# lam spread over partitions by a product with ones, and another order of the first weight chunks

## The chip, the cores and the metric

The kernel runs on one core of a Trainium2 chip. The metric is the device time of one execution, in microseconds (us), as the median of several runs. One further execution is recorded by the hardware profiler; all rows below are from that one.

## The reference, cut to what matters

The program is a linear attention with decay followed by two feed-forward layers, all in 32-bit floats. Inputs are q, k and v of 2 batches, 8 heads, 768 positions and 64 dimensions, one decay lam per head, and two pairs of weights.

```python
# per head, blocks of positions with a running state kv:
intra = (q_b @ k_b.T) * Dmask            # Dmask[i, j] = lam ** (i - j) for i >= j, else 0
out_b = intra @ v_b + (q_b * lam ** (pos + 1)) @ kv
kv    = lam ** block * kv + (k_b * lam ** (block - 1 - pos)).T @ v_b
x = out reshaped to 1536 tokens x 512
# layer 1 (w_in 512 x 2048, w_out 2048 x 512), ELU:
h = x @ w_in;  g = where(h > 0, h, exp(min(h, 0)) - 1);  x = g @ w_out
# layer 2, leaky with one slope alpha per hidden unit:
h = x @ w_in;  g = max(h, 0) + alpha * min(h, 0);         x = g @ w_out
```

## The kernel before, in words

The attention works on 12 blocks of 128 positions (6 per batch), all 8 heads of a block together. For block n, `scores(n)` (L201) multiplies keys and queries into two PSUM banks, `mask(n)` (L208, VectorE) multiplies them with the decay matrix `dm` into SBUF, `state(n)` (L223) multiplies the decayed keys `kd` (L182, GpSimd) with the values, `new_state(n)` (L235 ScalarE, L239 and L241 VectorE) updates the running state, and `outputs(n)` (L256 and, except in the first block of a batch, L262) adds what the block gives and what the state gives. `keep(n)` splits the output into a high part (L274, ScalarE) and a remainder (L275, VectorE), because the feed-forward products are made of three products of such parts in a reduced format.

The feed-forward part is a list of 96 items: layer, quarter of the hidden units, tile of 512 tokens, 128 hidden units. `up(i)` (L359) is 12 matmuls, then ScalarE's relu and exp (L370, L373), VectorE's `g` (L374), ScalarE's high part `gh` (L380) and GpSimd's remainder `gl` (L381). `down(i)` (L397) is 12 matmuls into four banks and runs two items later (`LAG`). PSUM has 8 banks in a ring, so a bank is reused once the tile eight allocations earlier is read.

Weights arrive in chunks of 1 MB. Chunk c = 2n is up weights (`wih`, `wil`) and c = 2n + 1 down weights (`woh`, `wol`) of the n-th pair of hidden units' groups: items 0 and 1 use chunk 0 in `up` and chunk 1 in `down`; items 2 and 3 use chunks 2 and 3. Three raw buffers hold them as they come. `split_w` converts one in six steps: a scaling on ScalarE (L125), a shift and two combining steps on VectorE (L126, L128, L131), the high part on ScalarE (L134) and the remainder on GpSimd (L135).

The order of each engine's instructions is the order in which they are written (`manual_schedule`); each engine works its own list in that order and waits where an operand isn't ready. A counter sets where a step of `split_w` stands: `tick()` advances it and issues what is due, `later(n, step)` makes a step due n ticks on. A block of the first four has three ticks between `block_a` and `block_b` and three behind; `up` has four, and an item four more in its `down`. So `split_w(c, gaps, first)` gives the ticks of the six steps, counted from where it is called:

```python
later(first, ...)     # ScalarE: scaling
later(gaps[0], ...)   # VectorE: shift
later(gaps[1], ...)   # VectorE: combining 1
later(gaps[2], ...)   # VectorE: combining 2
later(gaps[3], ...)   # ScalarE: high part
later(gaps[4], ...)   # GpSimd: remainder
```

`begin()` holds the start: lam is read three times in copies over partitions (L301, L304), blocks 0 to 3 and chunk 0 are loaded on SP's queue, PE runs up with 8 products of zeros (L281), and `dm` and `qp` (powers of lam) are built with scans on VectorE (L325, L330). The first four blocks (`AHEAD`) run by themselves; the other eight are laced into items 0 to 7, one each. `load(n + 4)` is issued behind block n, which frees its buffer, and `load_w` at places of its own, all on SP's queue.

Of the kernel before, what the change touches and what calls it, by code (L numbers as in the profile page):

```python
# [7 lines left out]
F32 = mybir.dt.float32  # L8
# [3 lines left out]
ALU = mybir.AluOpType  # L12

B, H, S, D = 2, 8, 768, 64
# [3 lines left out]
NP = H // 2  # L18
# [8 lines left out]
NG = 4  # L27
GF = NF // NG
LAG = 2
WARM = 8  # L30
AHEAD = 4


# [1 line left out]
def attention_two_layers(  # L35
# [13 lines left out]
    nc = tc.nc  # L49
# [3 lines left out]
    tiny = ctx.enter_context(tc.tile_pool(name="tiny", bufs=1))  # L53
# [12 lines left out]
    def bank(name):  # L66
        return ps.tile([128, 512], F32, tag="ps", name=name)

    alpha_sb = tiny.tile([128, NF], F32, name="alpha_sb")
    beta = tiny.tile([128, NF], F32, name="beta")  # L70
    warm = tiny.tile([128, C], F32, name="warm")
    anti = tiny.tile([128, C], F32, name="anti")
    lam_sb = tiny.tile([128, H], F32, name="lam_sb")
    lamp = tiny.tile([128, H], F32, name="lamp")
    fill = tiny.tile([128, 176], F32, name="fill")


    clock = [0]
# [2 lines left out]
    def later(n, step):  # L81
        if n:
            due.setdefault(clock[0] + n, []).append(step)
        else:
            step()
# [11 lines left out]
    def load_w(c):  # L97
        n, part = divmod(c, 2)
        l, k = divmod(n, NPAIR)
        wi, wo = wts[l]  # L100
        r = wraw.tile([128, 2048], U32, tag="raw", name="raw")
        if part == 0:
            nc.sync.dma_start(
                out=r.rearrange("p (c f) -> p c f", c=NCC),
                in_=wi[:, k * 512:(k + 1) * 512].rearrange("(c p) f -> p c f", p=128))
        else:
            nc.sync.dma_start(
                out=r.rearrange("p (f e) -> p f e", f=2),
                in_=wo[k * 256:(k + 1) * 256, :].rearrange("(f p) e -> p f e", p=128))
        raw[c] = r  # L110

    def split_w(c, gaps=(5, 6, 8, 11, 13), first=3):
        n, part = divmod(c, 2)
        r = raw.pop(c).rearrange("p (f w) -> p f w", w=2)


        upper, lower = r[:, :, 1], r[:, :, 0]
        t = wt.tile([128, 1024], F32, tag="wt", name="wt")
        tu = t.bitcast(U32)
        tag = "wi" if part == 0 else "wo"  # L120
        h = wsp.tile([128, 1024], F32R, tag=tag + "h", name=tag + "h")
        lo = wsp.tile([128, 1024], F32R, tag=tag + "l", name=tag + "l")
        shape = dict(c=NCC) if part == 0 else dict(c=2)
        split[c] = [x.rearrange("p (c f) -> p c f", **shape) for x in (h, lo)]
        later(first, lambda: nc.scalar.mul(t, upper.bitcast(F32), 2.0 ** -112))  # L125
        later(gaps[0], lambda: nc.vector.tensor_scalar(  # L126
            out=tu, in0=tu, scalar1=3, scalar2=None, op0=ALU.logical_shift_left))
        later(gaps[1], lambda: nc.vector.scalar_tensor_tensor(  # L128
            out=tu, in0=lower, scalar=29, in1=tu,
            op0=ALU.logical_shift_right, op1=ALU.bitwise_or))  # L130
        later(gaps[2], lambda: nc.vector.scalar_tensor_tensor(  # L131
            out=tu, in0=upper, scalar=0x80000000, in1=tu,
            op0=ALU.bitwise_and, op1=ALU.bitwise_or))
        later(gaps[3], lambda: nc.scalar.copy(h, t))  # L134
        later(gaps[4], lambda: nc.gpsimd.tensor_tensor(  # L135
            out=lo, in0=t, in1=h.bitcast(F32), op=ALU.subtract))
# [24 lines left out]
    def load(n):  # L161


        t = accp.tile([128, 4, 512], F32, tag="acc", name="blk")
        z = t[:, 0:2].rearrange("p s (a i) -> p s a i", a=NP)
        nc.sync.dma_start(out=z, in_=kqT[n])
        m = 2 if n % PB != PB - 1 else 1
        u = t[:, 2:4].rearrange("p s (h d) -> p s h d", h=H)
        nc.sync.dma_start(
            out=u[:, 0:m], in_=vk[n, :, 0:m, :].rearrange("j a (h d) -> j a h d", h=H))  # L170
        ld[n] = z
        vs[n] = (u[:, 0], u[:, 1] if m > 1 else None)
# [21 lines left out]
    def scores(n):  # L194
        z = ld[n]

        ps_ = [bank("sc"), bank("sc")]
        for pr in range(NP):
            for hs in range(2):
                a, b = hs * 64, (hs + 1) * 64  # L200
                nc.tensor.matmul(  # L201
                    out=ps_[hs][:, pr * C:(pr + 1) * C], lhsT=z[a:b, 0, pr, :],
                    rhs=z[a:b, 1, pr, :], start=True, stop=True)
        sc[n] = ps_

    def mask(n):
        for hs, p_ in enumerate(sc.pop(n)):
            nc.vector.tensor_tensor(  # L208
                out=sms[n % 2][:, hs], in0=p_.rearrange("p (a i) -> p a i", a=NP),
                in1=dm[:, hs], op=ALU.mult)  # L210
# [64 lines left out]
        nc.vector.tensor_tensor(  # L275
            out=xl[t][:, :, o:o + C], in0=pv, in1=xh_.bitcast(F32), op=ALU.subtract)

    def run_up():
        pw = bank("warm")
        for _ in range(WARM):  # L280
            nc.tensor.matmul(out=pw[:, 0:C], lhsT=warm, rhs=warm, start=True, stop=True)  # L281

    def block_a(n):
        p_ = state(n)
        if n + 1 < NBLK:
            scores(n + 1)
            mask(n + 1)
        return p_
# [8 lines left out]
            scale(n + 2)  # L297

    def begin():

        nc.sync.dma_start(out=lam_sb, in_=bass.AP(  # L301
            tensor=lam.tensor, offset=lam.offset, ap=[[0, 128], [1, H]]))
        for hs in range(2):
            nc.scalar.dma_start(out=lamp[hs * 64:(hs + 1) * 64, 0:NP], in_=bass.AP(  # L304
                tensor=lam.tensor, offset=lam.offset + hs, ap=[[0, 64], [2, NP]]))
        load(0)
        nc.scalar.dma_start(out=alpha_sb, in_=alpha)
        load(1)
        load_w(0)
        load(2)  # L310
        load(3)
        nc.vector.memset(warm, 0.0)
        run_up()

        nc.gpsimd.memset(anti, 0.0)
        nc.gpsimd.affine_select(
            out=anti, in_=anti, pattern=[[1, C]], base=1 - C, channel_multiplier=1,
            compare_op=ALU.not_equal, fill=1.0)
        nc.scalar.activation(fill[:, 0:1], warm[:, 0:1], AF.Exp)


        for hs in range(2):
            for pr in range(NP):
                h = 2 * pr + hs
                nc.vector.tensor_tensor_scan(  # L325
                    out=dm[:, hs, pr, :], data0=lam_sb[:, h:h + 1].to_broadcast([128, C]),
                    data1=anti, initial=0.0, op0=ALU.mult, op1=ALU.add)

        for pr in range(NP):
            nc.vector.tensor_tensor_scan(  # L330
                out=qp[:, pr, :], data0=lamp[:, pr:pr + 1].to_broadcast([128, C]),
                data1=warm, initial=1.0, op0=ALU.mult, op1=ALU.add)
        for s_ in st:
            nc.gpsimd.memset(s_, 0.0)
        scores(0)
        nc.vector.tensor_scalar(
            out=beta, in0=alpha_sb, scalar1=-1.0, scalar2=1.0, op0=ALU.mult, op1=ALU.add)
        scale(0)
        mask(0)
        scale(1)  # L340
        split_w(0, (3, 4, 5, 8, 9), 2)


    gh = {}
# [83 lines left out]
             for l in range(2) for q in range(NG) for t in range(NCH) for j in range(GF)]  # L428
    PER = NCH * GF

    when = {-1: [1], 0: [2], 2: [3]}
    early = {1: ((8, 9, 10, 12, 14), 7), 2: ((5, 6, 8, 9, 11), 2)}
    for g in range(1, 2 * NG):
        o = (g - 1) * PER

        a, b = (7, 8) if g == 1 else (2, 5)
# [3 lines left out]
    def weights(i):  # L440
        for c in when.get(i, []):
            split_w(c, *early.get(c, ()))
            if c + 3 < 4 * NPAIR:
                later(12 if c == 1 else 9, lambda c=c: load_w(c + 3))

    def parts(i, e):

# [3 lines left out]

    with tc.manual_schedule():
        begin()
        for n in range(AHEAD):
            weights(n - AHEAD)
            p_ = block_a(n)
            for _ in range(3):
                tick()
            block_b(n, p_)
            if n < 2:  # L460
                load_w(1 + n)
            if n == 3:
                load_w(3)
            for _ in range(3):
                tick()
        for i, _ in enumerate(items):
            n = AHEAD + i
            p_ = block_a(n) if n < NBLK else None
            up(i)
            weights(i)  # L470
            if n < NBLK:
                block_b(n, p_)
            for e in range(4):
                if i < LAG:
                    tick()
                else:
                    for c0, c1 in parts(i - LAG, e):
                        down(i - LAG, e, c0, c1)
        for i in range(len(items) - LAG, len(items)):
            for e in range(4):  # L480
                for c0, c1 in parts(i, e):
                    down(i, e, c0, c1)
# [50 lines left out]
```

## Time and profile before

| | us |
|---|---|
| median of 3 runs | 595.18 (594.75 to 597.2) |
| the profiled execution | 595.87 |
| its span, first to last instruction | 594.1 |
| PE (matmul) busy | 577.2, 97% of the span |
| VectorE (DVE) busy | 273.5, 46% |
| ScalarE (ACT) busy | 241.1, 41% |
| GpSimd (POOL) busy | 228.4, 38% |

Shares of busy time are averages over the whole span. The granted clock is TensorE's as a share of 2.4 GHz; its mean over the span is 0.986. A row of the chain of waits says what the work that ended last was waiting for or doing at that time. L12 is line 12 of the kernel before.

### The profile page before, as it was taken

How to read it: one execution, taken by the hardware profiler on the slowest of the kernel's cores; microseconds unless marked ns; L12 is line 12 of the kernel's file. 1: busy time of each engine (PE TensorE's matmuls, PEld its weight loads, DVE VectorE, ACT ScalarE, POOL GpSimd, SP SyncE). 2: the span in 40 equal slices, each digit the busy share in tenths (PEclk: the TensorE clock that was granted, in tenths of full speed). 3: DMA queues.
4: the chain of work that ended last, by engine and by line, in shares of the span. 5: the costliest groups of instructions: out<-in, count | busy, mean ns of one | idle time of the engine just before them, and what ended most of it. 6: DMA issues, size and time to landing. Idle time of an engine off the chain costs nothing.

```text
span 594.1 us, 7308 instructions
## 1 busy us (share of the span) xinstructions
PE 577.2 (97%) x2956; PEld 477.3 (80%) x2956; DVE 273.5 (46%) x359; ACT 241.1 (41%) x374; POOL 228.4 (38%) x156
## 2 busy tenths in 40 slices
PE   4897999999999999999999999999999999999997
PEld 4785778888888888888888888888888888888886
DVE  3786532656425435535526643443435532551332
ACT  1462444465445445454546533443324232422220
POOL 2648431354443443253344434353323344332211
PEclk7897999999999999999999999999999999999999
DMA  5995500242122222041022222122202110000111
GB/s 195 406 352 180 180 1 1 72 141 72 71 72 71 72 71 72 0 135 40 38 71 72 71 72 71 54 91 71 68 3 84 59 72 0 2 0 1 71 72 71
DMA packets 18993, 49.24 MB, mean 83 GB/s; under 512 B 1936, under 2 KB 2192, under 8 KB 18960
## 3 DMA queue, kind: packets, MB, share of 16 engines
q1 hardware_dynamic: 18272, 48.77, 23.6%
q8 instruction: 23, 0.38, 0.2%
q10 hardware_dynamic: 688, 0.01, 0.1%
q14 instruction: 10, 0.08, 0.0%
HBM read 45.63 MB, written 3.15 MB: 82 GB/s over the span
## 4 chain that ended last, share of the span: by engine, by line
PE 92%; DVE 3%; DMA 3%; ACT 1%; issue 0%; DVEq 0%; POOL 0%; POOLq 0%
PE up L359 44%; PE dn L397 44%; DMA raw<-in_w1i 2%; PE po L262 1%; PE po L256 1%; PE sc L201 1%; DMA lamp<-in_lam 1%; DVE wt L128 1%; DVE wt L131 1%; PE stp L223 1%; DVE acc L413 0%; ACT st L235 0%; ACT wt L125 0%; ACT wih L134 0%; DVE st L241 0%; DVE wt L126 0%
## 5 line engine op out<-in xcount | busy, mean ns | idle before, releaser
L381 POOL TENSOR_TENSOR gl_t<-g_t,gh_t 128x512 fp32r<-128x512 f32 x96 | 125.2, 1304 | 327.1 <-ACT gh_t L380 274.5
L370 ACT ACTIVATE r_t<-up 128x512 f32<-128x512 f32 x96 | 57.3, 597 | 197.0 <-PE up L359 197.0
L380 ACT CAST gh_t<-g_t 128x512 fp32r<-128x512 f32 x96 | 59.6, 621 | 108.8 <-DVE g_t L374 55.7
L413 DVE TENSOR_TENSOR acc<-dn,acc 128x512 f32<-128x512 f32 (+1 forms) x73 | 46.9, 676 | 75.7 <-PE dn L397 75.7
L397 PE MATMUL dn<-woh,gl_t 128*128 128x512 f32 (+1 forms) x196 | 75.4, 385 | 0.0
L397 PE MATMUL dn<-woh,gh_t 128*128 128x512 f32 (+1 forms) x196 | 75.4, 385 | 0.0
L397 PE MATMUL dn<-wol,gh_t 128*128 128x512 f32 (+1 forms) x196 | 75.4, 385 | 0.0
L378 DVE SCALAR_TENSOR_TENSOR g_t<-r_t,beta,up 128x512 f32<-128x512 f32 x48 | 35.7, 743 | 86.2 <-ACT r_t L370 77.5
L397 PE MATMUL dn<-gh_t,woh 128*128 128x512 f32 x192 | 75.3, 392 | 0.0
L397 PE MATMUL dn<-gl_t,woh 128*128 128x512 f32 x192 | 74.8, 389 | 0.0
L397 PE MATMUL dn<-gh_t,wol 128*128 128x512 f32 x192 | 74.7, 389 | 0.0
L374 DVE SCALAR_TENSOR_TENSOR g_t<-r_t,up 128x512 f32<-128x512 f32 x48 | 32.8, 683 | 63.1 <-ACT r_t L373 63.1
L359 PE MATMUL up<-xh,wih 128*128 128x512 f32 x192 | 53.1, 399 | 3.7 <-ACT wih L134 3.7
L359 PE MATMUL up<-xh,wil 128*128 128x512 f32 x192 | 52.2, 394 | 0.0
L359 PE MATMUL up<-xl,wih 128*128 128x512 f32 x192 | 52.2, 394 | 0.0
L359 PE MATMUL up<-yh,wih 128*128 128x512 f32 x192 | 51.3, 389 | 0.0
L359 PE MATMUL up<-yl,wih 128*128 128x512 f32 x192 | 51.3, 389 | 0.0
L359 PE MATMUL up<-yh,wil 128*128 128x512 f32 x192 | 51.3, 389 | 0.0
L359 PEld LDWEIGHTS up<-xh,wih 128*128 128x128 f32 x192 | 36.0, 190 | 11.8 <-ACT wih L134 3.9
L126 DVE TENSOR_SCALAR wt<-wt 128x1024 uint32<-128x1024 uint32 x32 | 30.0, 938 | 31.9 <-ACT wt L125 31.9
L359 PEld LDWEIGHTS up<-xh,wil 128*128 128x128 f32 x192 | 36.6, 191 | 7.8
L359 PEld LDWEIGHTS up<-xl,wih 128*128 128x128 f32 x192 | 36.6, 191 | 7.8
(52 smaller groups left out, 800.0 us busy)
## 6 DMA issues: line engine op xcount, KB each, us to landing
raw<-in_w1i SPq DMA_DIRECT2D x8, 1024.0 KB, 5.9
raw<-in_w1o SPq DMA_DIRECT2D x8, 1024.0 KB, 5.0
raw<-in_w2i SPq DMA_DIRECT2D x8, 1024.0 KB, 5.4
raw<-in_w2o SPq DMA_DIRECT2D x8, 1024.0 KB, 4.8
blk<-in_kqT SPq DMA_DIRECT2D x12, 512.0 KB, 6.1
blk<-in_vk SPq DMA_DIRECT2D x10, 512.0 KB, 7.0
out<-acc SPq DMA_DIRECT2D x11, 256.0 KB, 2.0
blk<-in_vk SPq DMA_DIRECT2D x2, 256.0 KB, 5.9
```

The lines of the kernel that those rows point to most:

```text
L126: later(gaps[0], lambda: nc.vector.tensor_scalar(out=tu, in0=tu, scalar1=3, scalar2=None, op0=ALU.logical_shift_left))
L128: later(gaps[1], lambda: nc.vector.scalar_tensor_tensor(out=tu, in0=lower, scalar=29, in1=tu, op0=ALU.logical_shift_right, op1=ALU.bitwise ...
L131: later(gaps[2], lambda: nc.vector.scalar_tensor_tensor(out=tu, in0=upper, scalar=0x80000000, in1=tu, op0=ALU.bitwise_and, op1=ALU.bitwise ...
L201: nc.tensor.matmul(out=ps_[hs][:, pr * C:(pr + 1) * C], lhsT=z[a:b, 0, pr, :], rhs=z[a:b, 1, pr, :], start=True, stop=True)
L359: nc.tensor.matmul(out=p_, lhsT=w[:, cc, fo:fo + 128], rhs=x[t][:, cc, :], start=n == 0, stop=n == 3 * NCC - 1)
L370: nc.scalar.activation(r, p_, AF.Relu, scale=-1.0)
L374: later(1, lambda: nc.vector.scalar_tensor_tensor(out=g, in0=r, scalar=-1.0, in1=p_, op0=ALU.add, op1=ALU.max))
L378: later(1, lambda: nc.vector.scalar_tensor_tensor(out=g, in0=r, scalar=beta[:, f:f + 1], in1=p_, op0=ALU.mult, op1=ALU.add))
L380: later(2, lambda: nc.scalar.copy(gh_, g))
L381: later(3, lambda: nc.gpsimd.tensor_tensor(out=gl_, in0=g, in1=gh_.bitcast(F32), op=ALU.subtract))
L397: nc.tensor.matmul(out=p_, lhsT=a, rhs=b, start=first and n == 0, stop=last and n == 2)
L413: nc.vector.tensor_tensor(out=a, in0=p_, in1=a, op=ALU.add)
```

## The change

lam is read once, as one row of 8 numbers on one partition. A matmul of a row of ones with it puts it on all 128 partitions; three copies on VectorE bring it into `lam_sb` and, for each half of the partitions, its even or odd heads into `lamp`. The run-up is three products ahead of that matmul and six behind it. alpha is loaded on SP's queue at item 2, and beta is made from it at item 20; both were in `begin()`. The conversion of chunk 0 has its first step one block later. Chunk 2 is loaded and converted ahead of chunk 1: its load comes behind block 0 and its conversion is called ahead of block 3; chunk 1's load comes behind block 1 and its conversion is called in item 0. `fill` is made smaller, so that the new row finds room.

```diff
-WARM = 8
...
+    row = tiny.tile([1, 128 + H], F32, name="row")
-    fill = tiny.tile([128, 176], F32, name="fill")
+    fill = tiny.tile([128, 40], F32, name="fill")
...
-    def run_up():
+    def run_up(n):
         pw = bank("warm")
-        for _ in range(WARM):
+        for _ in range(n):
             nc.tensor.matmul(out=pw[:, 0:C], lhsT=warm, rhs=warm, start=True, stop=True)
...
     def begin():
-        nc.sync.dma_start(out=lam_sb, in_=bass.AP(
-            tensor=lam.tensor, offset=lam.offset, ap=[[0, 128], [1, H]]))
-        for hs in range(2):
-            nc.scalar.dma_start(out=lamp[hs * 64:(hs + 1) * 64, 0:NP], in_=bass.AP(
-                tensor=lam.tensor, offset=lam.offset + hs, ap=[[0, 64], [2, NP]]))
+        nc.sync.dma_start(out=row[:, 128:128 + H], in_=lam.rearrange("h a -> a h"))
         load(0)
-        nc.scalar.dma_start(out=alpha_sb, in_=alpha)
         load(1)
         load_w(0)
         load(2)
         load(3)
         nc.vector.memset(warm, 0.0)
-        run_up()
+        nc.vector.memset(row[:, 0:128], 1.0)
...
+        run_up(3)
+
+        p_ = bank("lamp")
+        nc.tensor.matmul(
+            out=p_[:, 0:H], lhsT=row[:, 0:128], rhs=row[:, 128:128 + H], start=True, stop=True)
+        run_up(6)
+        nc.vector.tensor_copy(lam_sb, p_[:, 0:H])
+        for hs in range(2):
+            a, b = hs * 64, (hs + 1) * 64
+            nc.vector.tensor_copy(
+                lamp[a:b, 0:NP], lam_sb.rearrange("p (a s) -> p s a", s=2)[a:b, hs])
...
         scores(0)
-        nc.vector.tensor_scalar(
-            out=beta, in0=alpha_sb, scalar1=-1.0, scalar2=1.0, op0=ALU.mult, op1=ALU.add)
         scale(0)
         mask(0)
         scale(1)
-        split_w(0, (3, 4, 5, 8, 9), 2)
+        split_w(0, (5, 6, 7, 9, 11), 4)
...
-    when = {-1: [1], 0: [2], 2: [3]}
-    early = {1: ((8, 9, 10, 12, 14), 7), 2: ((5, 6, 8, 9, 11), 2)}
+    when = {-1: [2], 0: [1], 2: [3]}
+    early = {2: ((4, 5, 6, 8, 10), 3), 1: ((3, 4, 5, 7, 9), 2)}
...
-                later(12 if c == 1 else 9, lambda c=c: load_w(c + 3))
+                later(9, lambda c=c: load_w(c + 3))
...
             if n < 2:
-                load_w(1 + n)
+                load_w(2 - n)
...
         for i, _ in enumerate(items):
+            if i == 2:
+                nc.sync.dma_start(out=alpha_sb, in_=alpha)
+            if i == 20:
+                nc.vector.tensor_scalar(
+                    out=beta, in0=alpha_sb, scalar1=-1.0, scalar2=1.0, op0=ALU.mult,
+                    op1=ALU.add)
             n = AHEAD + i
```

## Rows read from the trace of the kernel before

**Rows 1.** The page's chain that ended last: shares of the span by engine.
```profile
PE 92%; DVE 3%; DMA 3%; ACT 1%; issue 0%; DVEq 0%; POOL 0%; POOLq 0%
```
**Rows 2.** Busy us of each engine in stretches, then granted clock, DMA share, GB/s.
```profile
5.00:10.00 5.00, 1.49 (x14) 1.50 (x16) 1.04 (x4) 0.83 (x2) 0.00 (x0) 0.86 0.50 183
10.00:15.00 5.00, 2.17 (x26) 1.76 (x26) 3.28 (x7) 0.00 (x0) 1.57 (x2) 0.50 1.03 405
15.00:20.00 5.00, 5.00 (x63) 4.71 (x60) 3.11 (x7) 1.74 (x2) 2.18 (x3) 0.62 1.03 420
...
100.00:580.00 480.00, 480.00 (x2137) 397.48 (x2136) 212.21 (x263) 201.06 (x296) 180.88 (x117) 1.00 0.18 60
```
**Rows 3.** The same view in stretches of 1 us, at 49 us.
```profile
49.00:50.00 1.00, 0.00 (x0) 0.00 (x0) 1.00 (x2) 0.23 (x1) 1.00 (x1) 0.78 0.08 33
```
**Rows 4.** Chain of waits in order of time, 0 to 60 us: start, us, what.
```profile
7.15 9.95 DMA raw<-in_w1i
...
17.12 1.15 ACT wt L125
...
24.09 1.04 ACT wih L134
...
27.38 1.14 PE po L262 x8
...
34.24 2.96 PE up L359 x12
...
42.42 1.16 ACT wt L125
...
44.47 3.28 DVE wt L128
...
49.77 1.05 ACT wih L134
...
50.87 5.49 PE up L359 x12
```
**Rows 5.** Timeline of PE: start, us, instructions, count [idle before, releaser].
```profile
8.51 2.03 PE L201 MATMUL sc<-blk 64*128 64x128 f32 x16 [3.67 <-DMA blk<-in_kqT]
...
16.43 1.97 PE L256 MATMUL po<-sm,blk 128*64 128x128 f32 x16
...
45.99 1.16 PE L201 MATMUL sc<-blk 64*128 64x128 f32 x16
```
**Rows 6.** Timeline of SP's queue: the issue of block 0's first half.
```profile
1.18 0.42 SPq L166 DMA_DIRECT2D blk<-in_kqT  x1
```
**Rows 7.** Transfers of tile blk issued in 56 to 60 us: issue to landing.
```profile
DMA to landing us min/median/max: 3.3/3.7/4.2
```
**Rows 8.** The page's DMA queues: packets, MB, share; this is ACT's queue.
```profile
q10 hardware_dynamic: 688, 0.01, 0.1%
```
**Rows 9.** Timeline of DVE: start, us, instructions, count [idle before, releaser].
```profile
3.41 2.63 DVE L325 TENSOR_TENSOR_SCAN dm<-lam_sb,anti 128x128 f32<-128x128 f32 x8 [2.41 <-DMA lam_sb<-in_lam]
11.72 2.19 DVE L330 TENSOR_TENSOR_SCAN qp<-lamp,warm 128x128 f32<-128x128 f32 x4 [5.67 <-DMA lamp<-in_lam]
...
13.88 1.28 DVE L208 TENSOR_TENSOR sm<-sc,dm 128x512 f32<-128x512 f32 x2
...
18.90 0.85 DVE L239 COPY st<-stp 64x256 f32<-64x256 f32 x2
19.79 0.69 DVE L275 TENSOR_TENSOR xl<-po,xh 128x512 fp32r<-128x512 f32 x1
...
36.69 1.22 DVE L128 SCALAR_TENSOR_TENSOR wt<-raw,wt 128x1024 uint32<-128x1024 uint32 x1
```
**Rows 10.** Timeline of POOL: start, us, instructions, count.
```profile
46.61 2.04 POOL L182 TENSOR_TENSOR kd_t<-blk,dm 128x512 f32<-128x512 f32 x1
...
71.68 2.41 POOL L135 TENSOR_TENSOR wol<-wt,woh 128x1024 fp32r<-128x1024 f32 x1
74.03 1.07 POOL L182 TENSOR_TENSOR kd_t<-blk,dm 128x512 f32<-128x512 f32 x1
```

## The prediction

> **What bounds the kernel now.** I read the chain of waits by engine and the busy times per stretch first. The chain lies on TensorE (PE) for 92% of the span [rows 1], and PE is busy for the whole of 100 to 580 us [rows 2]. Nothing in the change touches that part: the same matmuls run there behind the same conversions. So a gain or a loss must come from the first 60 us, and I read those in the chain of waits in order of time and then engine by engine.
>
> The chain there has three links to see [rows 4]. First, the first weight chunk (c = 0) is issued at 7.15 and lands 9.95 us later, at 17.1. Second, its conversion runs from 17.12 over ScalarE (ACT) and VectorE (DVE) to the copy at 24.09; the state update of block 1 is queued behind that copy, and PE's matmuls with this state start only at 27.38. From there PE runs with hardly a wait through up(0), 34.24 to 37.20. I call the end of up(0) U; it is 37.2. Third, chunk 2 (the second chunk of up weights): its conversion starts at 42.42 and ends with the copy at 49.77; PE has been idle since 47.15 [rows 5] and starts up(2) at 50.87. In that idle time the granted clock began to fall to its lower level, 1.2 of 2.4 GHz (0.78 on average in 49 to 50) [rows 3], and up(2) takes 5.49 us where up(0) took 2.96 [rows 4].
>
> Ahead of all this lies the transfer stream. It moves 183 GB/s between 5 and 10 us and 405 GB/s from 10 on [rows 2], and the first block, issued at 1.18 [rows 6], lets PE start at 8.51 only [rows 5].
>
> **The change part by part.** Times are of the profiled execution, 595.87 us.
>
> *lam as one row.* Three small transfers go (one of lam on SP, two on ACT), and alpha's leaves ACT's queue. Added are one row of 8 numbers, a memset of one row, a product with ones on PE, and three small DVE copies. The row stands first on SP, as lam does today, which has landed when the scans start at 3.41 [rows 9]; the trace doesn't show the row's own landing, and I take 3.4. For the product I take 0.4: a pair of f32 matmul records is 0.15 (16 in 1.16) at the full clock and 0.25 at the low one [rows 5], plus a hand-over. Each copy is at most one scan of 128 columns, 2.63/8 = 0.33 [rows 9], so 0 to 1.0 together, I take 0.6; the memset runs while DVE waits for the row. The eight scans then run from 4.4 to 7.0, and the four of qp follow at once to 9.2 with their 2.19, where today they wait for the transfer until 11.72. mask(0) ends at 10.5 with 1.28 [rows 9]. Of the run-up three products stand ahead of the lam product and six behind; these end at about 6.5 and delay only scores(0), which mask(0) doesn't need before 9.2.
>
> *The stream.* What I expect from this part is an earlier stream. The only sign in the trace is time: with the second queue's 688 small packets [rows 8] in flight the stream ran at less than half of its later rate [rows 2]. With an empty queue a block half lands 3.3 us after its issue [rows 7]; 0.52 MB at 405 GB/s are 1.3 of these. Block 0's first half, issued at 1.18, would then land at 4.5. Chunk 0 is the fifth load on SP, 3.15 MB with those ahead of it, 7.8 us of stream: it lands at 1.2 + 2.0 + 7.8 = 11.0. I allow 0.8 for a slow start and take 11.8 instead of 17.1. The bounds are 11.0 and the 17.1 of today.
>
> *Conversion of chunk 0 behind the first block.* Its first step (ACT) now stands behind ACT's copy of block 0's output, and its shift (DVE) behind mask(1), the state copies and the subtraction of block 0. So it can't start before that output: mask(0) at 10.5, the output matmuls (1.97 at the low clock [rows 5], half of it at the full one), one ACT copy (0.6, as half of the 1.04 for twice the columns [rows 4]): 12.1 to 13.1. From the start of the first step to the copy takes 6.97 today (17.12 to 24.09) [rows 4]; two state copies and a subtraction, 0.85 + 0.69, leave this stretch and mask(2), 1.28, comes in [rows 9]: 6.7. From the copy's start to the state matmuls of block 2 is 3.29 (24.09 to 27.38). So these start at 22.1 to 23.1 instead of 27.38. I take 23.1, since PE starts at the low clock: **4.2 us earlier**. The upper bound is 5.2. The lower is a stream as late as today: block 0's output at 18.4 (16.43 + 1.97) then holds the first step until 19.0, so the state matmuls come at 19.0 + 6.7 + 3.3 = 29.0, 1.6 later than today. Behind the shift that waits for chunk 0 DVE has mask(2), state(1) and mask(3) queued, so PE waits there in any case; at the full clock it would idle from 19 to 22.
>
> From there to U PE has its 9.8 us as today (27.38 to 37.20); the conversion of chunk 2, begun in block 3, lies beside it on ACT and DVE, and its last DVE step comes about when up(0) ends.
>
> *Up weights ahead of down weights.* Chunk 2 is loaded and converted before chunk 1. up(2) would start 9.9 behind U (47.15 − 37.20), and chunk 2 is done 1 to 4 us behind U, so the wait of 50.87 − 47.15 = 3.7 goes, and with it the low clock's 5.49 − 2.96 = 2.5: **6.2 us**. What is late next is chunk 1, the first down weights. Its conversion takes the very place that chunk 2's has today, behind item 0's g on ACT, 5.2 behind U (42.42 − 37.20). There chunk 2 was done with the copy 13.6 behind U (49.77 + 1.05). Its last two DVE steps took 5.3 (44.47 to 49.77) instead of 2 x 1.22 [rows 4, 9], while GpSimd (POOL) ran a subtraction, a kd and a qs product beside them (kd 2.04 instead of 1.07) [rows 10]. With only kd and qs beside them they take some 1.4 less (estimate); mask(6) now stands between them and costs some 0.7 net. So woh is ready 12.9 to 14.1 behind U (the later where the copy of chunk 2 holds up item 0's relu by up to 1.2), and wol 2.41 later [rows 10], at 15.3 to 16.5. down(0) comes at 9.9 + 2.96 + 1.0 = 13.9 and wants wol 0.45 later; its second bank waits for item 1's g, whose ACT steps queue behind woh, some 3 us after it (estimate: item 0's set with a state update took the 5.2 above). **New wait: 2.4 us**, bounds 0.5 (DVE undisturbed) and 6.3 (3.8, and the clock falling as at 49 to 50 for another 2.5). Chunks 3 and on keep their places.
>
> The trace shows a DVE step of two SBUF inputs stretched from 1.22 to 3.28 beside POOL [rows 4, 9]. The Trainium skill (SBUF — State Buffer, "Who interferes with whom") says that such an instruction shares a read interface with a GpSimd one that reads SBUF, and that one of them then blocks for the other's whole instruction. By that rule each step could wait out kd or qs in full and the new wait would be some 3.5; with the undisturbed 1.22 it would be 0.5. The rows lean to the rule.
>
> *alpha and beta.* alpha's issue moves to SP at item 2, behind a weight load that waits for chunk 1's buffer, and ahead of block 10's loads, needed three items later; beta (16 columns on DVE) to item 20. beta is used from item 48 on. PE's chain passes neither: 0; without that cover it would be one issue, 0.4 us [rows 6].
>
> **Sum.** 4.2 + 6.2 − 2.4 = 8.0 us: 595.87 − 8.0 = 587.9. The profiled execution is 0.7 above the median of the runs, 595.18, so I predict 587.2.
>
> **Rivals.**
> *The stream stays late* (it is slow at first by itself). For it: the second queue carried few bytes while the stream moved 183 GB/s [rows 2, 8]. Against it: an idle queue lands a block half in 3.3 us [rows 7]. Then −1.6 + 6.2 − 2.4 = 2.2: 593.0. The Trainium skill (DMA: Bandwidth & Descriptors, "Issuing engines are not separate DMA queues") says that all DMAs run on the same 16 engines and that issuing from several engines saves only issue time; by that rule leaving ACT's queue empty would give this rival's time, and the trace of before doesn't decide it.
> *The new wait is long*: woh late, PE idle long enough that the clock falls. 4.2 + 6.2 − 6.3 = 4.1: 591.1. For it: the clock fell 2.4 us into the idle time that begins at 47.15 [rows 3, 5]. Against it: the wait is cut in pieces by the matmuls with woh.
> *All fits*: 5.2 + 6.2 − 0.5 = 10.9: 584.3.
> *Slower, by the clock*: PE idles at the state matmuls of block 2, the clock falls there, and the gaps up to down(0) keep it low. Every us at the low level costs 0.43 to 0.5 (1.16 against 2.03 for scores) [rows 5]. It decides from 16 us of low clock on; 20 us give 595.2 − 8.0 + 10 = 597.2. For it: one spell, about 8.6 to 18.8, lasted 10 us (0.86, 0.50 and 0.62 in three stretches) [rows 2]. Against it: it ended once PE had work without gaps.
>
> **How the numbers follow.** Forecast 0.52, stream late 0.13, long wait 0.16, all fits 0.14, slower 0.05. The range goes from 582.5 (all fits, and 1.8 more for what the low clock cost before up(0)) to 593.5 (stream late, and 0.5 more wait). Half a per cent, what a measurement of this kernel tells from no change, is 3 us: faster (below 592.2) is the forecast, all fits, most of the long wait and a third of the late stream, 0.85; the same 0.11; slower 0.04.
>
> **What would show it.** Right: scores(0) start before 7 us, chunk 0's first step at 12 to 14, up(0) ends near 33, no wait of up(2), and waits of 1 to 4 us at down(0), first on wol or woh. Wrong: the stream's rate in 5 to 10 still near 183 GB/s; a granted clock below 1 behind 20 us; a wait of up(2); any new PE wait behind 70 us.

## The result, and the profile after

The changed kernel takes 587.08 us (median of 4 runs, 586.05 to 587.99) beside 596.19 us for the kernel before on the same chip (4 runs): a ratio of 0.9848, 95% interval 0.9815 to 0.9880. The profiled execution took 586.05 us with a span of 584.1; that of before took 595.87 with 594.1.

The stream of large loads starts at once. The stretches of the kernel after, with busy us of PE, PE's weight loads, DVE, ACT and POOL, then the granted clock, DMA share and GB/s, as in [rows 2]:

```profile
5.00:10.00 5.00, 4.97 (x60) 4.17 (x60) 5.00 (x12) 0.00 (x0) 1.47 (x2) 1.00 0.96 358
10.00:15.00 5.00, 2.73 (x44) 2.52 (x42) 4.01 (x7) 1.71 (x2) 1.95 (x3) 0.89 1.04 416
15.00:20.00 5.00, 5.00 (x62) 4.30 (x60) 3.20 (x4) 1.47 (x3) 4.95 (x4) 0.77 1.03 409
```

358 GB/s in 5 to 10 us stand against 183. Chunk 0 is also issued earlier, at 2.96 instead of 7.15. In the kernel before, the chain of waits begins with one of lamp's two transfers, and chunk 0's issue comes behind its landing (start, us, what):

```profile
0.74 6.39 DMA lamp<-in_lam
7.13 0.02 issue
7.15 9.95 DMA raw<-in_w1i
```

SP's queue waited twice for lamp to land, once with a half of block 2 (L169) and once with chunk 0 (L103); the kernel after has no such wait (us in total, times, longest):

```profile
SPq L169 <- DMA lamp<-in_lam: 2.6, 1, 2.6
...
SPq L103 <- DMA lamp<-in_lam: 1.1, 1, 1.1
```

The clock, recorded as low from 8.6 to 18.8 before, is recorded as low only from about 14 to 17 (0.89 and 0.77 in two stretches). PE's timeline (start, us, instructions, idle time before and what ended it) answers to [rows 5]; I add the steps at which the chain of the first 50 us can be read:

```profile
2.63 0.59 PE L317 MATMUL lamp<-row 1*128 1x8 f32 x2
...
6.01 1.65 PE L201 MATMUL sc<-blk 64*128 64x128 f32 x16
...
13.68 1.93 PE L201 MATMUL sc<-blk 64*128 64x128 f32 x16 [2.27 <-DMA blk<-in_kqT]
...
20.19 1.09 PE L256 MATMUL po<-sm,blk 128*64 128x128 f32 x16
21.82 1.13 PE L262 MATMUL po<-qs_t,st 128*128 128x128 f32 x8 [0.53 <-DVE st L241]
...
28.40 1.20 PE L362 MATMUL up<-xh,wih 128*128 128x512 f32 x4
...
41.33 1.19 PE L362 MATMUL up<-xh,wih 128*128 128x512 f32 x4
...
45.66 0.40 PE L400 MATMUL dn<-gl_t,woh 128*128 128x512 f32 x1
47.33 0.50 PE L400 MATMUL dn<-gh_t,wol 128*128 128x512 f32 x1 [1.28 <-POOL wol L135]
```

scores(0) start at 6.01 instead of 8.51, the state matmuls of block 2 at 21.82 instead of 27.38 [rows 4], up(0) at 28.40 instead of 34.24. up(2), at 41.33, has no wait. The 12 matmuls of the first down(0) begin at 45.3 and stop after two of them: the third wants `wol` and waits 1.28 us. All waits of PE, longest first (us in total, times, longest):

```profile
PE sc L201 <- DMA blk<-in_kqT: 2.3, 1, 2.3
PE dn L400 <- POOL wol L135: 1.3, 1, 1.3
PE warm L281 <- DVE warm L306: 1.1, 1, 1.1
PE po L262 <- DVE st L241: 0.5, 1, 0.5
```

VectorE's side of the start, and of chunk 1's conversion (answers to [rows 9]):

```profile
3.26 0.17 DVE L320 COPY lam_sb<-lamp 128x8 f32<-128x8 f32 x1 [2.13 <-PE lamp L317]
...
3.83 2.63 DVE L330 TENSOR_TENSOR_SCAN dm<-lam_sb,anti 128x128 f32<-128x128 f32 x8
6.38 2.16 DVE L335 TENSOR_TENSOR_SCAN qp<-lamp,warm 128x128 f32<-128x128 f32 x4
8.47 2.45 DVE L208 TENSOR_TENSOR sm<-sc,dm 128x512 f32<-128x512 f32 x4
...
20.79 0.88 DVE L241 TENSOR_TENSOR st<-stp,st 64x256 f32<-64x256 f32 x2 [2.29 <-ACT st L235]
...
39.47 1.96 DVE L128 SCALAR_TENSOR_TENSOR wt<-raw,wt 128x1024 uint32<-128x1024 uint32 x1
41.35 1.27 DVE L208 TENSOR_TENSOR sm<-sc,dm 128x512 f32<-128x512 f32 x2
42.55 1.21 DVE L131 SCALAR_TENSOR_TENSOR wt<-raw,wt 128x1024 uint32<-128x1024 uint32 x1
```

The copy of the lam product starts at 3.26, the scans follow without a wait, and the masks of blocks 0 and 1 begin at 8.47 instead of 13.88. ScalarE, where the first conversion begins behind the copy of block 0's output, and ends ahead of the state update:

```profile
10.90 0.58 ACT L274 CAST xh<-po 128x512 fp32r<-128x512 f32 x1 [8.67 <-PE po L256]
12.16 1.12 ACT L125 ACTIVATE wt<-raw 128x1024 f32<-128x1024 f32 x1 [0.68 <-DMA raw<-in_w1i]
18.53 1.05 ACT L134 CAST wih<-wt 128x1024 fp32r<-128x1024 f32 x1 [5.25 <-DVE wt L131]
...
43.80 1.05 ACT L134 CAST woh<-wt 128x1024 fp32r<-128x1024 f32 x1 [5.19 <-DVE wt L131]
```

and GpSimd beside chunk 1's conversion (answers to [rows 10]):

```profile
38.84 1.50 POOL L182 TENSOR_TENSOR kd_t<-blk,dm 128x512 f32<-128x512 f32 x1
40.31 2.27 POOL L189 TENSOR_TENSOR qs_t<-blk,qp 128x512 f32<-128x512 f32 x1
44.92 2.36 POOL L135 TENSOR_TENSOR wol<-wt,woh 128x1024 fp32r<-128x1024 f32 x1 [2.34 <-ACT woh L134]
```

### The profile page after: what moved, and what is told of

It reads as the page before. It is cut to its first block, busy times and chain, and to the rows that moved or that the text cites. A ratio compares the mean times of both kernels' runs of the same rounds, so it can differ in the third digit from the quotient of the medians.

```text
span 584.1 us, 7319 instructions
## 1 busy us (share of the span) xinstructions
PE 575.3 (98%) x2960; PEld 475.6 (81%) x2960; DVE 271.8 (47%) x363; ACT 240.9 (41%) x374; POOL 227.9 (39%) x156
## 4 chain that ended last, share of the span: by engine, by line
PE 93%; DVE 2%; DMA 2%; ACT 1%; POOL 0%; issue 0%; SPq 0%; DVEq 0%
PE dn L400 44%; PE up L362 43%; DMA raw<-in_w1i 2%; PE sc L201 1%; PE po L256 1%; PE po L262 1%; PE warm L281 1%; DVE wt L128 1%; PE stp L223 1%; ACT st L235 0%; DVE acc L416 0%; DVE wt L131 0%; POOL wol L135 0%; DVE st L241 0%; DVE wt L126 0%
## 5 line engine op out<-in xcount | busy, mean ns | idle before, releaser
L400 PEld LDWEIGHTS dn<-gh_t,wol 128*128 128x128 f32 x192 | 36.0, 188 | 9.2 <-POOL wol L135 1.7
L400 PEld LDWEIGHTS dn<-woh,gl_t 128*128 128x128 f32 x196 | 36.8, 188 | 7.4
L400 PEld LDWEIGHTS dn<-wol,gh_t 128*128 128x128 f32 x196 | 36.8, 188 | 7.4
```

The lines of the kernel that those rows point to most:

```text
L400: nc.tensor.matmul(out=p_, lhsT=a, rhs=b, start=first and n == 0, stop=last and n == 2)
```

## The experiments

Each was timed beside the kernel before on the same chip; ratios are to it. Diffs are against the changed kernel. The first four ask where the gain comes from.

**Lamp's two element-wise transfers back (e1_lamp_back).**

```diff
+        for hs in range(2):
+            nc.scalar.dma_start(out=lamp[hs * 64:(hs + 1) * 64, 0:NP], in_=bass.AP(
+                tensor=lam.tensor, offset=lam.offset + hs, ap=[[0, 64], [2, NP]]))
...
-        for hs in range(2):
-            a, b = hs * 64, (hs + 1) * 64
-            nc.vector.tensor_copy(
-                lamp[a:b, 0:NP], lam_sb.rearrange("p (a s) -> p s a", s=2)[a:b, hs])
```

> The changed kernel with lamp loaded again by the two element-wise transfers on ACT's queue (the two copies into lamp left out); alpha stays late on SP. Theory A, that these small transfers hold up the stream of large loads: scores(0) start at about 8.5 again instead of 6.0, the stream moves under 250 GB/s in 5 to 10 us instead of 358, the first step of chunk 0 comes at 17 or later instead of 12.2, the end of up(0) is 4 to 6 us later, and the time is 591 to 594. Rival, that the stream was late for another reason (lam's broadcast on SP, alpha, or by itself): stream and chunk 0 as in the changed kernel, only qp waits for lamp, time within 1 us of 587.

Measured: 596.23 us, ratio 0.9991 (0.9976 to 1.0006). The whole gain is gone, more than theory A expected. The stretch and PE's timeline show both halves of the loss:

```profile
5.00:10.00 5.00, 2.70 (x20) 2.40 (x20) 1.17 (x4) 0.00 (x0) 0.00 (x0) 1.00 0.50 190
```

```profile
8.38 2.08 PE L201 MATMUL sc<-blk 64*128 64x128 f32 x16 [2.30 <-DMA blk<-in_kqT]
...
30.11 2.05 PE L262 MATMUL po<-qs_t,st 128*128 128x128 f32 x8 [4.20 <-DVE st L241]
```

190 GB/s and scores(0) at 8.38 are the kernel before again. The state matmuls of block 2 come at 30.11, later than the 27.38 of before, at the low clock (2.05 instead of 1.13) and behind a wait of 4.2 us: with a late stream the new places of the conversions cost what the new order brings.

**Alpha back on ACT's queue (e2_alpha_back).** 

```diff
+        nc.scalar.dma_start(out=alpha_sb, in_=alpha)
...
-            if i == 2:
-                nc.sync.dma_start(out=alpha_sb, in_=alpha)
```

> The changed kernel with alpha's load again on ACT's queue behind block 0's loads. Theory A, that it is lamp's 512 single elements that hold up the stream: alpha is 128 rows of 64 bytes, so the loss is under 1 us: chunk 0's first step by 13, time 587 to 588. Rival, that any small transfer on a second queue does it: chunk 0's first step at 14 to 17, time 589 to 592.

Measured: 585.74 us, ratio 0.9826 (0.9801 to 0.9850), not to be told from the changed kernel. Chunk 0's first step is at 11.75. A small load on the second queue is harmless; the move of alpha is worth nothing.

**The new order alone (e3_order_only).** Against the kernel before:

```diff
-        split_w(0, (3, 4, 5, 8, 9), 2)
+        split_w(0, (5, 6, 7, 9, 11), 4)
...
-    when = {-1: [1], 0: [2], 2: [3]}
-    early = {1: ((8, 9, 10, 12, 14), 7), 2: ((5, 6, 8, 9, 11), 2)}
+    when = {-1: [2], 0: [1], 2: [3]}
+    early = {2: ((4, 5, 6, 8, 10), 3), 1: ((3, 4, 5, 7, 9), 2)}
...
-                later(12 if c == 1 else 9, lambda c=c: load_w(c + 3))
+                later(9, lambda c=c: load_w(c + 3))
...
-                load_w(1 + n)
+                load_w(2 - n)
```

> The kernel before with the new order and places of the weight conversions alone, lam and alpha loaded as before. By the prediction's sum: chunk 0's first step at about 19, the state matmuls of block 2 at 29 (1.6 later than before), no wait of up(2), a wait of 1 to 3 us at down(0): 592 to 594. Rival, that the new order alone gives most of the gain since PE's 6.2 us at up(2) are lost to nothing else: 588 to 590.

Measured: 595.41 us, ratio 0.9992 (0.9978 to 1.0006). No gain: 2 us less than the prediction's sum for this case. The waits of PE:

```profile
PE po L262 <- DVE st L241: 4.2, 1, 4.2
...
PE dn L397 <- POOL wol L135: 1.3, 1, 1.3
```

The wait of up(2) is gone and that of down(0) is 1.3, as in the sum. But the state matmuls of block 2, at 28.70 as forecast (29.0), come behind a wait of 4.2 us in which the clock falls (0.74 and 0.58 in 25 to 35 us), and up(0) starts at 37.76, 3.5 later than before (34.24): 1.3 from the late state matmuls, which the sum had as 1.6, and 2.2 from the low clock behind them, which it left out.

**The lam change alone (e4_lam_only).** The same lines, in the changed kernel as they were before:

```diff
-        split_w(0, (5, 6, 7, 9, 11), 4)
+        split_w(0, (3, 4, 5, 8, 9), 2)
...
-    when = {-1: [2], 0: [1], 2: [3]}
-    early = {2: ((4, 5, 6, 8, 10), 3), 1: ((3, 4, 5, 7, 9), 2)}
+    when = {-1: [1], 0: [2], 2: [3]}
+    early = {1: ((8, 9, 10, 12, 14), 7), 2: ((5, 6, 8, 9, 11), 2)}
...
-                later(9, lambda c=c: load_w(c + 3))
+                later(12 if c == 1 else 9, lambda c=c: load_w(c + 3))
...
-                load_w(2 - n)
+                load_w(1 + n)
```

> The changed kernel with the old order and places of the weight conversions; lam's row, the product and alpha stay changed. By the prediction's sum: the stream is early, up(0) ends at 31 to 33 instead of 37.2, the wait of up(2) of about 3.7 us and its low clock (2.5 us) stay: 590 to 592. Rival, that the wait of up(2) was an effect of the late start and goes with it: 586 to 588.

Measured: 590.96 us, ratio 0.9907 (0.9884 to 0.9930). up(0) starts at 29.00, and the wait of up(2) is there with its old length:

```profile
PE up L362 <- ACT wih L134: 3.7, 1, 3.7
```

So alone the lam change brings 0.9% and the new order nothing measurable, and together they bring 1.5%: the new order pays only where the stream is early.

The next question is what it is in lamp's transfers.

**No product: lam as 128 copies of its row (e5_broadcast).**

```diff
-        nc.sync.dma_start(out=row[:, 128:128 + H], in_=lam.rearrange("h a -> a h"))
+        nc.sync.dma_start(out=lam_sb, in_=bass.AP(
+            tensor=lam.tensor, offset=lam.offset, ap=[[0, 128], [1, H]]))
...
-        p_ = bank("lamp")
-        nc.tensor.matmul(
-            out=p_[:, 0:H], lhsT=row[:, 0:128], rhs=row[:, 128:128 + H], start=True, stop=True)
...
-        nc.vector.tensor_copy(lam_sb, p_[:, 0:H])
```

> The changed kernel without the product: lam comes as 128 copies of its row of 32 bytes, first on SP's queue as in the kernel before, and lamp is copied from it on VectorE. Theory: what held up the stream were lamp's 512 single elements and nothing else, so the stream is as early as in the changed kernel (over 340 GB/s in 5 to 10 us, chunk 0's first step by 12.7) and the time is 586 to 588; the product itself is worth nothing. Rival: any load of lam in many small pieces holds up the stream, so 128 pieces cost a quarter of 512 or more: chunk 0 at 13.5 or later, 589 or more.

Measured: 587.09 us, ratio 0.9853 (0.9824 to 0.9883). The stream moves 415 GB/s in 5 to 10 us. The product with ones is worth nothing; that lamp is copied from `lam_sb` instead of loaded is worth all that the lam change brings.

**The element-wise transfers on SP's queue (e11_lamp_sp).** 

```diff
+        for hs in range(2):
+            nc.sync.dma_start(out=lamp[hs * 64:(hs + 1) * 64, 0:NP], in_=bass.AP(
+                tensor=lam.tensor, offset=lam.offset + hs, ap=[[0, 64], [2, NP]]))
...
-        for hs in range(2):
-            a, b = hs * 64, (hs + 1) * 64
-            nc.vector.tensor_copy(
-                lamp[a:b, 0:NP], lam_sb.rearrange("p (a s) -> p s a", s=2)[a:b, hs])
```

> As e1_lamp_back, but lamp's two element-wise transfers are issued on SP's own queue, ahead of block 0. Theory, that it is the single elements whatever queue they are on: the stream starts late again, chunk 0's first step at 17 or later, 593 to 597. Rival, that it is two queues taking turns: on one queue the elements pass first and the stream then runs at its full rate, chunk 0's first step at 13 to 15, 587 to 590.

Measured: 596.11 us, ratio 0.9999 (0.9981 to 1.0017). Block 0's first half is issued at 2.56, and the stretches show when its bytes move:

```profile
4.00:6.00 2.00, 1.96 (x10) 1.77 (x9) 2.00 (x7) 0.00 (x0) 0.00 (x0) 1.00 0.04 0
6.00:8.00 2.00, 0.00 (x0) 0.00 (x0) 0.17 (x1) 0.00 (x0) 0.00 (x0) 1.00 0.10 21
8.00:10.00 2.00, 0.00 (x0) 0.00 (x0) 0.44 (x2) 0.00 (x0) 0.00 (x0) 0.78 0.94 377
```

Next to nothing moves until about 8 us, then the stream has its full rate: on one queue the pieces pass first, as the rival had it, but they take so long that the loss is the same (chunk 0's first step is at 18.86). It is the pieces, not the second queue.

**The same two transfers in 128 pieces (e12_lamp_rows).** Four numbers side by side for each partition, so lamp holds other heads than the reference wants. Against e1_lamp_back:

```diff
-                tensor=lam.tensor, offset=lam.offset + hs, ap=[[0, 64], [2, NP]]))
+                tensor=lam.tensor, offset=lam.offset + hs * NP, ap=[[0, 64], [1, NP]]))
```

> As e1_lamp_back (two transfers into lamp on ACT's queue), but each partition gets four numbers that lie side by side, so 128 pieces of 16 bytes instead of 512 of 4; lamp then holds the wrong heads, everything else is as in the changed kernel. Theory, that the number of single pieces is what holds up the stream: over 320 GB/s in 5 to 10 us, chunk 0's first step by 13.5, 586 to 589. Rival, that it is these two transfers as such (half the partitions each, ACT's queue): as e1_lamp_back, under 250 GB/s, 593 or more.

Measured: 587.96 us, ratio 0.9878 (0.9837 to 0.9919). 369 GB/s in 5 to 10 us, chunk 0's first step at 12.77. ACT's queue in the first 12 us of e1_lamp_back and of this kernel (packets, MB, share):

```profile
q10 hardware_dynamic: 544, 0.00, 2.1%
```

```profile
q10 hardware_dynamic: 160, 0.00, 0.6%
```

With the same bytes on the same queue, 544 packets cost the 9 us and 160 about 1 or nothing. So the cause is that lamp was loaded in single elements. Whether it is their number or their size of 4 bytes isn't shown: the two change together here.

The rest asks for the conversions.

**Chunk 0 at its old place (e6_c0_old_place).** 

```diff
-        split_w(0, (5, 6, 7, 9, 11), 4)
+        split_w(0, (3, 4, 5, 8, 9), 2)
```

> The changed kernel with the conversion of chunk 0 at its old place, ahead of block 0's output. Theory, that with an early stream this place matters little, since chunk 0 lands at about 12 when block 0's output is just done: state matmuls of block 2 at 21.5 to 22.5, 586.5 to 588. Rival, that moving it behind the first block was worth what it cost in the late stream (some 1.5 us): 588.5 or more.

Measured: 586.86 us, ratio 0.9848 (0.9824 to 0.9872): the changed kernel's. With the early stream the place behind the first block is worth nothing. What it costs with the late one was not tried by itself.

**Chunk 1's conversion a tick earlier (e7_down_early).**

```diff
-    early = {2: ((4, 5, 6, 8, 10), 3), 1: ((3, 4, 5, 7, 9), 2)}
+    early = {2: ((4, 5, 6, 8, 10), 3), 1: ((2, 3, 5, 7, 9), 1)}
```

> The changed kernel with the first steps of chunk 1's conversion one tick earlier, so that its scaling on ScalarE stands ahead of gh(0) and its shift ahead of the remainder of item 0. Theory, that the remaining wait of 1.3 us at down(0) hangs on this chain: the wait goes or falls under 0.4, 585.5 to 586.5. Rival, that VectorE is held by GpSimd's products beside it and takes longer: the wait stays over 0.8 and the time is that of the changed kernel.

Measured: 584.72 us, ratio 0.9812 (0.9791 to 0.9833). All waits of PE:

```profile
PE sc L201 <- DMA blk<-in_kqT: 1.8, 1, 1.8
PE warm L281 <- DVE warm L306: 1.1, 1, 1.1
PE po L262 <- DVE st L241: 0.7, 1, 0.7
```

The wait of down(0) is gone, and the time is 0.8 us below the theory's range. The intervals of the two ratios overlap a little, so of the 2 us between them the wait's 1.3 is what the profile shows. The scaling runs at 34.69 instead of 37.44, in a gap that ScalarE has ahead of gh(0).

**Block 2 ahead of chunk 0 (e9_k2_late_c0).**

```diff
+        load(2)
...
-        load(2)
...
-        split_w(0, (5, 6, 7, 9, 11), 4)
+        split_w(0, (11, 12, 13, 16, 17), 10)
```

> The changed kernel with block 2's loads ahead of chunk 0's, and chunk 0's conversion six ticks later (behind block 1), so that it doesn't hold the state update of block 1. Theory: scores(2) start at 11.5 instead of 13.7, the clock doesn't fall at 14 to 17, block 2 no longer waits, and up(0) starts 1.5 to 3 us earlier: 584 to 585.5. Rival, that the stream bounds this stretch (chunk 2 and blocks 4 and 5 land as before): up(0) less than 1 us earlier, 586 to 587.

Measured: 585.10 us, ratio 0.9827 (0.9803 to 0.9851). scores(2) start at 11.27 instead of 13.68 without a wait, the clock stays at 1.00 and up(0) starts at 25.25, 3.2 us earlier. Of these 1.0 comes out at the end (583.1 of span against 584.1), and by the times alone the two kernels can't be told apart. Down(0) now waits 2.8 in two pieces instead of 1.3, and block 6's output matmuls just ahead of it take 1.65 instead of 1.09 (at 41.12), held by mask(6), which ends at 41.63:

```profile
PE dn L400 <- POOL wol L135: 1.7, 1, 1.7
PE dn L400 <- ACT woh L134: 1.1, 1, 1.1
```

**Both, with chunk 2 a tick later (e10_all).** Against e9_k2_late_c0:

```diff
-    early = {2: ((4, 5, 6, 8, 10), 3), 1: ((3, 4, 5, 7, 9), 2)}
+    early = {2: ((5, 6, 7, 9, 11), 4), 1: ((2, 3, 5, 7, 9), 1)}
```

> Block 2's loads first and chunk 0's conversion behind block 1 as in e9_k2_late_c0, chunk 1's one tick earlier as in e7_down_early, and chunk 2's one tick later, so that its wait for the load doesn't hold the output of block 3. Theory: the two gains add up, 582 to 583.5. Rival, that they collide (chunk 2 later holds chunk 1 and down(0) waits again): 584 to 586.

Measured: 585.06 us, ratio 0.9821 (0.9795 to 0.9847): the rival's time. `woh` is ready in time, but down(0) waits 2.4 us for `wol`. The chain of waits (start, us, what) runs over GpSimd, where `wol` is queued behind block 7's two products:

```profile
40.07 2.14 POOL kd_t L182
42.21 1.25 POOL qs_t L189
43.46 2.32 POOL wol L135
...
45.83 2.56 PE dn L400 x10
```

**The best version (e13_best).** e9 with chunk 1's two combining steps ahead of mask(6) and its remainder ahead of these products.

```diff
-        load_w(0)
         load(2)
+        load_w(0)
...
-        split_w(0, (5, 6, 7, 9, 11), 4)
+        split_w(0, (11, 12, 13, 16, 17), 10)
...
-    early = {2: ((4, 5, 6, 8, 10), 3), 1: ((3, 4, 5, 7, 9), 2)}
+    early = {2: ((4, 5, 6, 8, 10), 3), 1: ((2, 3, 4, 5, 7), 1)}
```

> Block 2's loads first and chunk 0's conversion behind block 1 as in e9_k2_late_c0, chunk 2 at its place in the changed kernel; of chunk 1's conversion the first step one tick earlier as in e7_down_early, both combining steps ahead of mask(6) and the remainder on GpSimd ahead of the two products of block 7. Theory, that in e9 and e10 chunk 1's chain (VectorE behind mask(6), GpSimd behind kd and qs) was all that kept down(0): its wait falls from 2.8 to under 0.5, 582 to 583.5. Rival, that mask(6) or kd come late in turn, or the stream bounds: 584 to 585.5.

Measured: 582.25 us (5 runs, 582.10 to 582.72), ratio 0.9774 (0.9755 to 0.9794), clearly better than the changed kernel. The waits of PE that are left:

```profile
PE sc L201 <- DMA blk<-in_kqT: 1.7, 1, 1.7
PE warm L281 <- DVE warm L306: 1.1, 1, 1.1
```

In this execution block 3's scores still waited 1.7 us for their load and the clock fell behind it (0.78 in 15 to 20 us); there the stream bounds.

## Why the prediction was right, point by point

It forecast 587.2; 587.08 was measured. That the point is so near is in part luck: the kernel before ran at 596.19 beside it, 1.0 above the median that the forecast started from, so the gain is 9.1 us where 8.0 were summed. In the two profiled executions it is 9.8, nearer to the 10.9 of the rival "all fits" than to 8.0. The places and the signs of all three terms held; two sizes were off, and both were too cautious.

*The start, 4.2 us.* It is 5.6 at the state matmuls of block 2 (27.38 to 21.82) and 5.8 at the start of up(0), above the upper bound of 5.2. The stream was sized rightly: chunk 0 was there at 12.1, put at 11.8. Its cause was not: the prediction calls time the only sign in the trace, but the chain of before begins with lamp's transfer, and SP's queue waits for it twice. The step that was sized wrongly is the choice between 12.1 and 13.1 for the conversion's start: I took the later, with block 0's output matmuls at the low clock. scores(1), at 8.30, ran in 1.16 us, so the clock was up by then; the row of lam had also landed when its product started at 2.63, not at 3.4. Block 0's output was copied at 10.90, and the conversion started with chunk 0's landing, at 12.16. From there it took 6.37 (6.7 forecast) to the copy at 18.53 and 3.29 (3.29) to the state matmuls. The wait of scores(2) for block 2, 2.27 us with a low clock behind it, is not in the prediction; it lay beside this chain: mask(2) lost 0.3 by it. The term's place in the sum was right: e4_lam_only has it alone, and 590.96 lies in the 590 to 592 expected.

*The wait of up(2), 6.2 us.* It went in full: no wait of up(2) and no low clock behind 20 us. e4_lam_only, with the old order, still has its 3.7 us.

*The new wait, 2.4 us.* It is 1.3 us, at the place named, on `wol`. Up(0) ends at 31.4; `woh` was ready 13.5 behind that (12.9 to 14.1 forecast), `wol` 15.9 (15.3 to 16.5) and down(0) began 13.9 behind it (13.9). What was too large is the part for the second bank: its matmuls followed those of the first at 47.67 without a wait. scores(8), at 50.44, took 0.4 us longer than others. e7_down_early takes the wait away. In the kernel after, the whole of down(0) takes 1.6 us longer than before (45.32 to 49.83, against 57.34 to 60.28). So the terms as measured make 5.8 + 6.2 − 1.6 − 0.4 = 10.0, which is the difference of the two spans (594.1 and 584.1); the profiled executions differ by 9.8.

*The port.* The first combining step of chunk 1 took 1.96 us, neither 1.22 nor 3.28, while kd beside it took 1.50 instead of 1.07 and qs 2.27 instead of 1.29. So both engines were stretched, as [rows 4] and [rows 10] show of before. By the rule of the Trainium skill (SBUF — State Buffer, "Who interferes with whom") one waits out the other's whole instruction. The trace agrees in the order of the ends: kd ended at 40.34, the step 1.09 later and qs 1.15 behind that, each a little less than its length alone; before, the step ended at 47.75 [rows 4] and kd 0.90 behind it [rows 10]. The 0.7 us lost here are less than the price that the prediction gave for that rule, a kd or a qs in full, which fits that kd had begun at 38.84, 0.63 ahead of the step. No run set the rule against an even sharing.

*The rivals.* "The stream stays late" is answered by e1_lamp_back and e11_lamp_sp: it was late because of lamp's pieces. The Trainium skill (DMA: Bandwidth & Descriptors, "Issuing engines are not separate DMA queues") says that DMAs run on the same 16 engines whichever engine started them. The trace agrees: on the other queue the pieces cost the same (596.11 in e11_lamp_sp, 596.23 in e1_lamp_back). But the change doesn't move the pieces to another queue, it takes them away, so the rule didn't speak for this rival. What bears on it stands elsewhere on that page of the Trainium skill ("Rules for kernel authors"): a strided last dimension becomes one descriptor for each element. The trace agrees with 544 packets in e1_lamp_back against 160 in e12_lamp_rows, and I had not used it. That rival's own time, 593.0, was too good as well: e3_order_only, which is this case, took 595.4, because PE's 4.2 us of waiting at the state matmuls bring the clock down. That is the place and the mechanism of the rival "slower, by the clock"; it stops at no change.

What each edit is worth is now shown: that lamp is copied on VectorE and not loaded in single elements is the condition for everything; the new order adds 0.6% to that (0.9848 against 0.9907); the product with ones, alpha's place and chunk 0's place add nothing that can be measured. Beta's place and the longer run-up were not tried by themselves.

## What to carry to other kernels

Look at the first microseconds of the transfer stream: a load of 2 KB in 512 pieces of 4 bytes held up all large loads behind or beside it for about 5 us, while with 128 pieces of 16 to 64 bytes chunk 0's conversion began within 0.6 us of the changed kernel's (11.65 to 12.77 against 12.16). Change the access pattern or copy on chip before changing queues, and look in the chain of waits for a small transfer ahead of a large one. An order of steps is worth what the stretch allows in which it stands: moving work off PE's path paid nothing while the stream was late, and 0.6% once it was early.

## What the runs showed of the hardware

Pieces of 4 bytes cost far more than their bytes. On SP's queue alone the 512 of e11_lamp_sp, issued at 1.15, kept the queue's next bytes back until about 8 us. On ACT's queue beside the stream, in e1_lamp_back, they halved its rate to 190 GB/s in 5 to 10 us. They also held back SP's queue: in the kernel before, the issues of block 1's halves took 2.07 and 1.69 us where 0.43 is usual in the kernel after, and chunk 0 was issued at 7.15, against 2.96 after and 3.18 in e12_lamp_rows. Chunk 0's landing doesn't follow its issue, though: with lamp's single elements in flight it is at 17.0 to 17.1, whether the issue is at 5.60 (e1_lamp_back), 6.76 (e11_lamp_sp) or 7.15 (before). By then the stream has moved 3.7 to 4.0 MB, as it has by 12.1 in the kernel after (3.7). So what counted for chunk 0 was the bytes that the stream had not moved early on.

The recorded granted clock reads 1.00 from the first microsecond on, but the run-up products took 0.24 us for each record (2.93 us for 12 in the kernel after), near the 0.26 of the state matmuls, of the same shape, at the low level (2.05 for 8 in e1_lamp_back) and not the 0.14 at the high one (1.13 for 8). scores(0) took 1.65 us where the same 16 records later took 1.16. So ahead of its first change the record doesn't tell the level, and the durations do. In the kernel before the run-up's 16 records took 3.79 us, 0.24 each, so PE was at the low level ahead of the spell that the prediction puts at 8.6 to 18.8, too.
